# Attention numerators with tokens on partitions, quotients turned back by TensorE, and a planner with another product pace

## The chip, the cores and the metric

The kernel runs on one core of one Trainium2 chip. The metric is the device time of one execution in microseconds (us), lower is better; before the change the median of 3 runs is 940.74 us (940.22 to 941.93).

## The reference

```
def phi(x):                       # x: q or k, scaled by 64 ** -0.25
    proj = einsum('bhsd,md->bhsm', x, omega)
    h = proj - sum(x * x, -1) / 2
    return exp(h - max(h, -1)) / sqrt(m)
kv  = einsum('bhsm,bhsd->bhmd', k_p, v);  z = sum(k_p, axis=2)
num = einsum('bhsm,bhmd->bhsd', q_p, kv)
den = einsum('bhsm,bhm->bhs', q_p, z)[..., None] + 1e-06
x = (num / den) as 2304 tokens x 512
x = (silu(x @ w_gate) * (x @ w_val)) @ w_out        # 512 -> 1536 -> 512
x = g(x @ w_in) @ w_out2                            # 512 -> 2048 -> 512, g piecewise quadratic
```

Batch is 4, heads 8, sequence 576, head size 64, features m = 128. Everything is float32.

## The kernel before, in words

The 2304 tokens are cut into nine blocks of 256 (`TB`), numbered k; the eight heads into two halves of four heads, numbered d. So there are 18 pieces (k, d) of attention output.

**Attention.** `front` (L616 to L670) makes exp(features) of keys or queries with tokens on partitions: TensorE projects (L639), VectorE takes the negated maximum (L648), ScalarE the exponential (L661, or L665 on VectorE and L669). `k_group` multiplies these with the values, 65 columns a head: 64 values and a column of ones whose sum becomes z (L708). `kv_evac` copies the finished sums of a batch into `kvr`, once the 64 columns of kv, once z repeated over 64 columns. `q_group` turns the queries' features so that features lie on partitions (L779, TensorE transposes against the identity `ids`, copied to `q_t`).

**The piece that changes.** `num` makes the output of one piece with the kv sums as the stationary operand: for each of two head pairs it sends the 256 turned queries through `kvr`'s kv half and through its z half (L833, eight products of 256 columns; 16 shorter ones where a block crosses from one batch into the next, at k = 2, 4 and 6). So the numerator stands in one PSUM bank with head dimensions on partitions, and the denominator, repeated over 64 partitions, in another. `norm` inverts the denominator on VectorE: transpose in 32 x 32 blocks (L796), a strided sum that adds 1e-6 (L798), a reciprocal of 16 columns (L800), a transpose back (L801), and the product with the numerator (L805). The result `os` is split into a high and a low part (`x1s`, through `parts`) and stored to `x1d`.

**The two dense layers.** Each product is made of three matmuls (L403 to L405, high x high, high x low, low x high), 256 columns each. The first two sixths of layer one run as soon as a block is ready (`moe1`), between the pieces of attention. The rest runs in passes (`late_up`, `late_down`): `set_up` makes seven products a set in Strassen's manner on sums of input quarters, with partial sums copied from PSUM into the tile `eb` (`keep_bank`, the copy is L384 on ScalarE or L386 on VectorE) and added there (L1235); the products after them in the same bank wait for that copy. Weights come as raw 64-bit numbers: a transfer into `ws`, then L420 on ScalarE and L421 to L427 on VectorE make float32 of them (`to_f32`), a store to `w32` for later.

**What sets the order.** A planner (`Planner`) runs the whole program once while it is recorded: every step of every process gets a cost (`c_pe`, `c_act`, `c_dve`, fixed numbers) and a priority (the `PR_` numbers), and the time at which the planner's clock dispatches it fixes its place in its engine's queue. Engines take their queues strictly in that order, whatever the chip's real pace. `SLACK_D` is the time that `late_down` lets pass after an output row is ready before it plans the products on that row. All transfers are issued by SyncE (SP), also in planned order.

Of the kernel before, what the change touches and what calls it, by code (L numbers as in the profile page):

```python
# [19 lines left out]
F32 = mybir.dt.float32  # L20
F32R = mybir.dt.float32r
U32 = mybir.dt.uint32
AF = mybir.ActivationFunctionType
ALU = mybir.AluOpType
AX = mybir.AxisListType
# [3 lines left out]
P = 128  # L29
TB = 256  # L30
# [9 lines left out]
LEAN_A, LEAN_B, POOL_B = 0.97, -0.09, 5.00  # L40
ALT = 1.63

SLACK_D, SLACK_U = 3.0, 0.8

O_OFF, P_OFF, H_OFF = 32, 48, 48

NWL, NB1 = 7, 8
KINS, VINS, QINS, EBK, EBQ, N_QT = 3, 5, 2, 3, 2, 3
N_KL, N_QL, N_EL = 2, 1, 1

GROUPS = ((0,), (1, 2), (3, 4), (5, 6), (7, 8))

# [6 lines left out]
N_WT, N_XU = 3, 2  # L59
N_EB, N_GB, N_HL, N_HB, N_XI = 4, 2, 2, 1, 4  # L60

PR_K, PR_Q0, PR_Q = (0.32, 0.77, 0.91, 1.17), 0.17, 0.68
PR_C0, PR_C, PR_CS = 0.66, 1.02, 1.13
PR_W = 1.06
PR_BANK = 0.3
PR_FRONT = 0.35
PR_ST, PR_X, PR_E = 1.50, 0.74, 1.45
T_V, T_Q0, T_C0 = 3.0, 3.5, 7.0
N_GATE, N_CS = 1, 6
N_WS = 2  # L70

ORDER = (0, 1, 2, 3, 4)
# [61 lines left out]
class Planner:  # L134
# [24 lines left out]
    def set(self, ev):  # L159
        ev.done = True  # L160
        ev.src = self.src()
        for p in ev.waiters:
            self.after(p, ev.src)
            self.push(self.now, self.step, p, None)
        ev.waiters = []
# [93 lines left out]
def c_act(n, bias=False):  # L259
    return (115 + n) / 1200.0 + (0.05 if bias else 0.0)  # L260


def c_dve(n, psum=False, fast=False):
    return (66 + (n / 2 if fast else n)) / 960.0


def c_pool(n):
    return 0.11 + 0.00218 * n


def c_pe(n):
    return max(0.109, 0.0045 + n * 0.000442)


@with_exitstack
def performer_moe_kernel(ctx: ExitStack, tc: tile.TileContext, qX, kX, vX, om, ident,
                         w1, wo1, w2, wo2, out):
    nc = tc.nc
    pl = Planner()
# [4 lines left out]
    def bufs(pool, name, n, shape, dt=F32):  # L284
        return [pool.tile(shape, dt, tag=f"{name}{i}", name=f"{name}{i}") for i in range(n)]

    def ring(*a):
        return Ring(bufs(*a))
# [6 lines left out]
    bank = ring(psum, "bank", 8, [P, 512])  # L295
# [32 lines left out]
    osb = ring(keep, "os", 3, [P, 512])  # L328
# [5 lines left out]
    att_cm = tc.tile_pool(name="att", bufs=1, side="right", reuse_waits="tile")  # L334
    att = att_cm.__enter__()
    stat = ring(att, "st", 10, [P, 8, 4])
    rec = ring(att, "rec", 2, [P, 512])
    rect = ring(att, "rect", 1, [P, 16, 33])
    vin = ring(att, "vi", VINS, [P, 390])
    qts = ring(att, "qt", N_QT, [P, 2, 2, TB])  # L340
    ids = att.tile([P, P], F32, name="ids")
# [3 lines left out]
    ebufs = {False: ring(att, "ebk", EBK, [P, 2, 512]), True: ring(att, "ebq", EBQ, [P, 2, 512])}  # L345
    kin = ring(att, "ki", KINS, [P, 2, 512])
    qin = ring(att, "qi", QINS, [P, 2, 512])
    kvr = {(b, d): att.tile([P, 2, 2, P], F32, name=f"kvr{b}_{d}") for b in range(4) for d in range(2)}
    lent_cm = tc.tile_pool(name="lent", bufs=1, side="left", reuse_waits="tile")
    lent = lent_cm.__enter__()  # L350
    lent_ids = set()
# [1 line left out]
    def lend(rng, *a):  # L353
        for t in bufs(lent, *a):
            rng.free.append((t, None))
            lent_ids.add(id(t))
            lent_keep.append(t)
# [12 lines left out]
    lend(kin, "kl", N_KL, [P, 2, 512])  # L370
    lend(qin, "ql", N_QL, [P, 2, 512])
    lend(ebufs[False], "el", N_EL, [P, 2, 512])
    nc.gpsimd.memset(rect.free[0][0][:, :, 32:33], 1e-6)


    def dma(dst, src, nbytes):
        yield Op("SP", 0.06, lambda: nc.sync.dma_start(dst, src))
        yield Op("HW", 0.05, None)
        yield Op("DMA", nbytes / 330e3, None)

    def copy(dst, src, n, sbuf=True, scale=None):
        e = pl.pick(ACT=c_act(n), DVE=c_dve(n, fast=sbuf))
        if e == "ACT":
            yield Op("ACT", c_act(n), lambda: nc.scalar.activation(dst, src, AF.Copy, scale=1.0 if scale is None else scale))  # L384
        elif scale is None:
            yield Op("DVE", c_dve(n, fast=sbuf), lambda: nc.vector.tensor_copy(dst, src), sbuf)  # L386
        else:
            yield Op("DVE", c_dve(n, fast=sbuf), lambda: nc.vector.tensor_scalar(
                out=dst, in0=src, scalar1=scale, scalar2=None, op0=ALU.mult))
# [190 lines left out]
    halves = slice(0, 64), slice(64, P)  # L580

    def bank_pair():

        tok = yield Get(two_banks)
        b0 = yield Get(bank)
        b1 = yield Get(bank)
        pl.put(two_banks, tok)
        return b0, b1
# [30 lines left out]
    def front(xb, n, loads, is_q, rng):  # L619
# [13 lines left out]
        rank = pl.cur.rank  # L633
        pl.cur.rank = min(pl.cur.prio, PR_FRONT)

# [47 lines left out]
    def k_group(b, gs, kb, prev):  # L683
# [28 lines left out]
        for u in range(2 * n):  # L712
            i = 2 * gs[0] + u
            if i % 9 == 8:
                pl.spawn(kv_evac(b, i // 9), pl.cur.prio - 0.1)
# [22 lines left out]
    def kv_evac(b, d):  # L738
        kb = kv_bank.pop((b, d))
        kp = kb.rearrange("p (u c) -> p u c", c=P)  # L740
        kz = kvr[b, d].rearrange("p r a c -> p (r a) c")
        yield from copy(kz[:, :, 0:64], kp[:, :, 0:64], 256, False, 1.0 / P)
        yield from copy(kz[:, :, 64:P], kp[:, :, 64:65].to_broadcast([P, 4, 64]), 256, False, 1.0 / P)
        pl.put(bank, kb)
        pl.set(kv_ready[b, d])

# [41 lines left out]
            yield ev  # L788
        pl.spawn(num(k, d, q_t), pl.cur.prio - 0.05)

    def norm(pn, pd, rc, x):

        tt = yield Get(rect)
        st = yield Get(stat)
        s = st.rearrange("p a b -> p (a b)")
        yield Op("DVE", c_dve(512), lambda: nc.vector.transpose(out=tt[:, :, 0:32], in_=pd.rearrange("p (n c) -> p n c", c=32)))  # L796
        pl.put(bank, pd)
        yield Op("DVE", 0.105, lambda: nc.vector.tensor_reduce(out=s[:, 0:16], in_=tt[:, :, 0:33:32], axis=AX.X, op=ALU.add))  # L798
        pl.put(rect, tt)
        yield Op("DVE", 0.14, lambda: nc.vector.reciprocal(out=s[:, 16:32], in_=s[:, 0:16]))  # L800
        yield Op("DVE", c_dve(512), lambda: nc.vector.transpose(  # L801
            out=rc.rearrange("p (n c) -> p n c", c=32), in_=s[:, 16:32].unsqueeze(2).to_broadcast([P, 16, 32])))
        pl.put(stat, st)
        if pl.pick(DVE=c_dve(512), POOL=c_pool(512) + c_act(512) + ALT) == "DVE":
            yield Op("DVE", c_dve(512), lambda: nc.vector.tensor_tensor(out=x, in0=pn, in1=rc, op=ALU.mult))  # L805
            pl.put(bank, pn)
        else:
            yield Op("ACT", c_act(512), lambda: nc.scalar.activation(x, pn, AF.Copy))
            pl.put(bank, pn)
            yield Op("POOL", c_pool(512), lambda: nc.gpsimd.tensor_tensor(out=x, in0=x, in1=rc, op=ALU.mult))  # L810

    def num(k, d, q_t):
        yield x1_have[k]
        cuts = []
        t0 = k * TB
        while t0 < (k + 1) * TB:
            b = t0 // 576
            t1 = min((b + 1) * 576, (k + 1) * TB)
            cuts.append((b, t0 - k * TB, t1 - k * TB))
            t0 = t1  # L820
        for b, _, _ in cuts:
            yield kv_ready[b, d]
        x = yield Get(osb)
        rc = yield Get(rec)
        banks = yield from bank_pair()
        pl.cur.rank = min(pl.cur.prio, PR_FRONT)

        def mm():
            for r in range(2):
                for what in range(2):  # L830
                    for b, c0, c1 in cuts:
                        for a, h in enumerate(halves):
                            nc.tensor.matmul(banks[what][h, r * TB + c0:r * TB + c1], kvr[b, d][:, r, a, halves[what]],  # L833
                                             q_t[:, r, a, c0:c1], start=True, stop=True, skip_group_check=True)
        yield Op("PE", 1.88 if len(cuts) == 1 else 1.94, mm)
        pl.put(qts, q_t)
        yield from norm(*banks, rc, x)
        pl.put(rec, rc)
        pl.cur.rank = PR_Q
        yield from x1_split(k, d, x)  # L840
        yield from dma(half_block(x1d, k, d), x.rearrange("p (n t) -> p n t", n=2), P * 512 * 4)
        pl.put(osb, x)

    def half_block(t, k, d):

        return t[k // 2][:, 2 * d:2 * d + 2, (k % 2) * TB:(k % 2 + 1) * TB]

    def x1_split(k, d, x):
        xs = x1_tile[k]
        hi, lo = (xs[:, l, 2 * d:2 * d + 2].rearrange("p k t -> p (k t)") for l in range(2))  # L850
        yield from parts(hi, lo, x, 512)
        x1_cnt[k] = x1_cnt.get(k, 0) + 1
        if x1_cnt[k] == 2:
            pl.set(x1_ready[k])
# [808 lines left out]
```

## Time and profile before

| | |
|---|---|
| median of 3 runs | 940.74 us |
| the profiled execution | 939.58 us, its span 937.8 us |
| PE (TensorE matmuls) | 927.0 us busy, 99% |
| DVE (VectorE) | 787.0 us, 84% |
| ACT (ScalarE) | 509.2 us, 54% |
| POOL (GpSimd) | 65.1 us, 7% |
| PE's granted clock | 0.999 of full speed (2.4 GHz) |
| DMA | 147.68 MB, mean 157 GB/s |

The span is what the profiler covers of the profiled execution; 1.8 us of that execution lie outside it. The attention pieces lie in its first 232 us, mixed with products of the first layer from 47 us on; the rest is dense layers. A busy TensorE is counted from the start of a matmul to its modelled end, and these overlap, so a busy share of 100% hides short waits: the number of matmuls that start in a stretch tells more.

### The profile page before, as it was taken

What the parts mean: (1) busy time and instruction counts of PE and PEld (TensorE: products, weight loads), DVE (VectorE), ACT (ScalarE), POOL (GpSimd) and SP (SyncE); (2) the same over time, 40 slices, a digit from 0 to 9 for tenths busy, and PEclk for the clock granted to TensorE, in tenths of its full rate; (3) what the DMA queues carried; (4) which work ended last, traced back from release to release, by engine and by line L of the source; (5) the groups of instructions that cost most, each with busy time, mean ns of one, the idle gap of its engine ahead of it and who ended that gap; (6) DMA issues with size and microseconds to landing.
All of it is one profiled execution on the core that took longest, in us unless ns stands there. A gap on an engine that the chain in (4) does not pass through costs nothing.

```text
span 937.8 us, 22182 instructions
## 1 busy us (share of the span) xinstructions
PE 927.0 (99%) x8980; PEld 902.7 (96%) x8980; DVE 787.0 (84%) x1483; ACT 509.2 (54%) x1126; POOL 65.1 (7%) x57
## 2 busy tenths in 40 slices
PE   8999999999999999999999999999999999999998
PEld 7889899999999999999999999999999999999998
DVE  6899988778889999999989999997697678866553
ACT  7889975543446545564445465554455445544331
POOL 0332226222100000000000000000000000000000
PEclk9999999999999999999999999999999999999999
DMA  7667566555576366756745745442323031303022
GB/s 244 202 201 233 183 223 198 186 180 184 199 239 211 129 208 215 249 179 194 231 149 192 251 142 172 145 157 76 118 68 114 33 114 46 135 13 102 1 91 91
DMA packets 88663, 147.68 MB, mean 157 GB/s; under 512 B 8304, under 2 KB 43888, under 8 KB 88560
## 3 DMA queue, kind: packets, MB, share of 16 engines
q1 hardware_dynamic: 88560, 146.26, 47.8%
q8 instruction: 70, 1.15, 0.5%
q14 instruction: 33, 0.27, 0.1%
HBM read 103.24 MB, written 42.99 MB: 156 GB/s over the span
## 4 chain that ended last, share of the span: by engine, by line
PE 76%; DVE 15%; DMA 4%; issue 2%; ACT 2%; SPq 1%; DVEq 0%; ACTq 0%
PE bank L403 23%; PE bank L404 22%; PE bank L405 22%; PE bank L639 3%; PE bank L833 3%; PE bank L779 1%; PE bank L708 1%; DMA xq<-x2d 1%; DMA ws<-in_w_dram 1%; DVE st L648 1%; DVE x1s L396 1%; DVE wt L427 1%; DVE wt L425 1%; DMA ws<-in_wo_dram 1%; DVE xq L396 1%
## 5 line engine op out<-in xcount | busy, mean ns | idle before, releaser
L403 PE MATMUL bank<-x1s,w 128*128 128x256 f32 x492 | 137.4, 279 | 0.4 <-DVE eb L1235 0.4
L405 PE MATMUL bank<-x1s,w 128*128 128x256 f32 x492 | 136.1, 277 | 0.0
L404 PE MATMUL bank<-x1s,w 128*128 128x256 f32 x492 | 136.0, 276 | 0.0
L403 PEld LDWEIGHTS bank<-x1s,w 128*128 128x128 f32 x492 | 92.4, 188 | 1.6 <-DVE eb L1235 0.6
L405 PEld LDWEIGHTS bank<-x1s,w 128*128 128x128 f32 x492 | 92.5, 188 | 0.0
L404 PEld LDWEIGHTS bank<-x1s,w 128*128 128x128 f32 x492 | 92.4, 188 | 0.0
L403 PE MATMUL bank<-x1s,wb 128*128 128x256 f32 x286 | 79.2, 277 | 1.7 <-ACT eb L384 1.0
L384 ACT ACTIVATE x1s<-xq 128x512 fp32r<-128x512 f32 x80 | 50.2, 629 | 54.1 <-PE bank L405 23.2
L405 PE MATMUL bank<-x1s,wb 128*128 128x256 f32 x286 | 79.0, 276 | 0.0
L404 PE MATMUL bank<-x1s,wb 128*128 128x256 f32 x286 | 79.0, 276 | 0.0
L403 PE MATMUL bank<-x1s,wx 128*128 128x256 f32 x278 | 77.2, 278 | 1.0 <-ACT eb L384 1.0
L404 PE MATMUL bank<-x1s,wx 128*128 128x256 f32 x278 | 76.8, 276 | 0.0
L405 PE MATMUL bank<-x1s,wx 128*128 128x256 f32 x278 | 76.8, 276 | 0.0
L396 DVE TENSOR_TENSOR x1s<-xq,x1s 128x512 fp32r<-128x512 f32 x90 | 61.9, 687 | 9.0 <-ACT x1s L384 8.5
L384 ACT ACTIVATE eb<-bank 128x512 f32<-128x512 f32 x94 | 55.6, 591 | 23.6 <-PE bank L405 23.2
L420 ACT ACTIVATE wt<-ws 128x512 f32<-128x512 f32 x68 | 46.3, 686 | 35.4 <-DMA ws<-in_w_dram 18.3
L648 DVE TENSOR_REDUCE st<-bank 128x4 f32<-128x512 f32 (+1 forms) x76 | 47.9, 655 | 11.2 <-PE bank L639 11.2
L403 PEld LDWEIGHTS bank<-x1s,wb 128*128 128x128 f32 x286 | 53.7, 188 | 2.1 <-ACT eb L384 1.2
L384 ACT ACTIVATE hlr<-hb 128x512 fp32r<-128x512 f32 x53 | 33.4, 632 | 41.0 <-PE bank L404 26.2
L404 PEld LDWEIGHTS bank<-x1s,wb 128*128 128x128 f32 x286 | 53.7, 188 | 0.0
L405 PEld LDWEIGHTS bank<-x1s,wb 128*128 128x128 f32 x286 | 53.7, 188 | 0.0
L403 PEld LDWEIGHTS bank<-x1s,wx 128*128 128x128 f32 x278 | 52.2, 188 | 1.4 <-ACT eb L384 1.2
(256 smaller groups left out, 3341.6 us busy)
## 6 DMA issues: line engine op xcount, KB each, us to landing
ws<-in_w_dram SPq DMA_DIRECT2D x40, 512.0 KB, 4.7
ws<-in_wo_dram SPq DMA_DIRECT2D x28, 512.0 KB, 4.3
xq<-x1d SPq DMA_DIRECT2D x36, 256.0 KB, 4.2
xq<-x2d SPq DMA_DIRECT2D x36, 256.0 KB, 4.1
qi<-in_qX_dram SPq DMA_DIRECT2D x28, 256.0 KB, 3.8
ki<-in_kX_dram SPq DMA_DIRECT2D x22, 256.0 KB, 3.9
x1d<-os SPq DMA_DIRECT2D x18, 256.0 KB, 3.8
op<-os SPq DMA_DIRECT2D x18, 256.0 KB, 2.0
```

The lines of the kernel that those rows point to most:

```text
L384: yield Op("ACT", c_act(n), lambda: nc.scalar.activation(dst, src, AF.Copy, scale=1.0 if scale is None else scale))
L396: yield Op("DVE", c_dve(n), lambda: nc.vector.tensor_tensor(out=dst, in0=a, in1=b, op=op), True)
L403: nc.tensor.matmul(ps, l_hi, r_hi, start=first, stop=False, skip_group_check=shared)
L404: nc.tensor.matmul(ps, l_hi, r_lo, start=False, stop=False, skip_group_check=shared)
L405: nc.tensor.matmul(ps, l_lo, r_hi, start=False, stop=last, skip_group_check=shared)
L420: yield Op("ACT", 0.575, lambda: nc.scalar.activation(t, hw.bitcast(F32), AF.Abs))
L425: yield Op("DVE", c_dve(512), lambda: nc.vector.scalar_tensor_tensor(out=ti, in0=lw, scalar=29, in1=ti, op0=ALU.logical_shift_right, op1=A ...
L427: yield Op("DVE", c_dve(512), lambda: nc.vector.scalar_tensor_tensor(out=ti, in0=hw, scalar=0xC0000000, in1=ti, op0=ALU.bitwise_and, op1=A ...
L639: nc.tensor.matmul(banks[a][:, u * P:(u + 1) * P], xb[h, l, u * P:(u + 1) * P], r[h], start=first and (last or u == 0), stop=last, skip_gr ...
L648: yield Op("DVE", c_dve(256 * n), lambda: nc.vector.tensor_reduce(out=sv[:, a, units, 3 if by_pe else 0], in_=pv[a], axis=AX.X, op=ALU.max ...
L708: nc.tensor.matmul(kp[h, 2 * pr + a, 0:65], es[:, a, u * P + 64 * m:u * P + 64 * m + 64], v[:, 65 * a:65 * a + 65], start=(li == 0 and a = ...
L833: nc.tensor.matmul(banks[what][h, r * TB + c0:r * TB + c1], kvr[b, d][:, r, a, halves[what]], q_t[:, r, a, c0:c1], start=True, stop=True, ...
```

## The change

The numerators are computed with the operands exchanged. The turned queries become the stationary operand (64 tokens of one head at a time), and `kvr`, now 65 columns a head (kv and z side by side, one copy instead of two), is sent through them: 16 matmuls of 65 columns a piece, whatever batch border it crosses. So numerator and denominator stand with tokens on partitions: for each of the two banks (128 tokens each) VectorE adds 1e-6 to four columns, one reciprocal serves 8 columns, and one product a bank writes the quotients to `rec`. Four TensorE transposes turn them back, and a copy (16 of 18 on ScalarE) brings them to `os`. The tile `rect` and GpSimd's part in the quotient go.

The planner's price of a product changes (0.1177 to 0.1134 us for 256 columns), `SLACK_D` from 3.0 to 2.0, some priorities and start times, and three lent buffers become five (`N_KL`, `N_EL`).

```diff
-SLACK_D, SLACK_U = 3.0, 0.8
+SLACK_D, SLACK_U = 2.0, 0.8
-N_KL, N_QL, N_EL = 2, 1, 1
+N_KL, N_QL, N_EL = 3, 1, 2
-PR_K, PR_Q0, PR_Q = (0.32, 0.77, 0.91, 1.17), 0.17, 0.68
+PR_K, PR_Q0, PR_Q = (0.32, 0.9, 0.96, 1.0), 0.17, 1.01
-T_V, T_Q0, T_C0 = 3.0, 3.5, 7.0
-N_GATE, N_CS = 1, 6
+T_V, T_Q0, T_C0 = 3.84, 2.87, 5.5
+N_GATE, N_CS = 1, 3
...
 def c_pe(n):
-    return max(0.109, 0.0045 + n * 0.000442)
+    return max(0.109, n * 0.1134 / 256)
...
     def kv_evac(b, d):
-        kz = kvr[b, d].rearrange("p r a c -> p (r a) c")
-        yield from copy(kz[:, :, 0:64], kp[:, :, 0:64], 256, False, 1.0 / P)
-        yield from copy(kz[:, :, 64:P], kp[:, :, 64:65].to_broadcast([P, 4, 64]), 256, False, 1.0 / P)
+        yield from copy(kvr[b, d], kp[:, :, 0:65], 260, False, 1.0 / P)
...
-    def norm(pn, pd, rc, x):
+    def norm(pn, xt):
...
+        pv = [ps[:, 0:260].rearrange("p (h c) -> p h c", c=65) for ps in pn]
+        for t in range(2):
+            yield Op("DVE", 0.12, lambda: nc.vector.tensor_scalar(
+                out=s[:, 4 * t:4 * t + 4], in0=pv[t][:, :, 64], scalar1=1e-6, scalar2=None, op0=ALU.add))
+        yield Op("DVE", 0.12, lambda: nc.vector.reciprocal(out=s[:, 8:16], in_=s[:, 0:8]))
+        for t in range(2):
+            yield Op("DVE", c_dve(TB), lambda: nc.vector.tensor_tensor(
+                out=xt[:, t].rearrange("p (h c) -> p h c", c=64), in0=pv[t][:, :, 0:64],
+                in1=s[:, 8 + 4 * t:12 + 4 * t].unsqueeze(2).to_broadcast([P, 4, 64]), op=ALU.mult))
+            pl.put(bank, pn[t])
...
         def mm():
+            for t in range(2):
+                for h in range(4):
+                    for m, rows in enumerate(halves):
+                        nc.tensor.matmul(banks[t][rows, 65 * h:65 * h + 65], q_t[:, h // 2, h % 2, t * P + 64 * m:t * P + 64 * m + 64],
+                                         kvr[tiles[t][m], d][:, h], start=True, stop=True, skip_group_check=True)
+        yield Op("PE", 1.02, mm)
+        pl.put(qts, q_t)
+        yield from norm(banks, xt)
+        tp = yield Get(bank)
+
+        def trans():
             for r in range(2):
-                for what in range(2):
-                    for b, c0, c1 in cuts:
-                        for a, h in enumerate(halves):
-                            nc.tensor.matmul(banks[what][h, r * TB + c0:r * TB + c1], kvr[b, d][:, r, a, halves[what]],
-                                             q_t[:, r, a, c0:c1], start=True, stop=True, skip_group_check=True)
-        yield Op("PE", 1.88 if len(cuts) == 1 else 1.94, mm)
...
+                for t in range(2):
+                    nc.tensor.transpose(tp[:, r * TB + t * P:r * TB + (t + 1) * P], xt[:, t, r * P:(r + 1) * P], ids)
+        yield Op("PE", 0.55, trans)
+        pl.put(rec, xt)
+        x = yield Get(osb)
+        yield from copy(x, tp, 512, False)
```

How the queues change is read from the built programs. On PE, at the two pieces of the last token block (`bank<-qt,kvr` are the numerators and denominators, `hl,w` the dense layers' products), before:

```order
L405 MATMUL bank_64<-hl,w_114 128x256
L833 MATMUL bank_65<-qt_140,kvr_0_163 64x256 x2
L833 MATMUL bank_68<-qt_140,kvr_0_163 64x256 x2
L833 MATMUL bank_65<-qt_140,kvr_0_163 64x256 x2
L833 MATMUL bank_68<-qt_140,kvr_0_163 64x256 x2
L833 MATMUL bank_69<-qt_142,kvr_1_164 64x256 x2
```

and at the same place in the changed program (with `ids,rec`, the transposes, further down):

```order
L403 MATMUL bank_66<-hl,w_114 128x256
L819 MATMUL bank_70<-kvr_0_162,qt_140 64x65 x8
L819 MATMUL bank_64<-kvr_0_162,qt_140 64x65 x8
L819 MATMUL bank_68<-kvr_1_163,qt_141 64x65 x8
L819 MATMUL bank_67<-kvr_1_163,qt_141 64x65 x8
L401 MATMUL bank_66<-hl,w_115 128x256
...
L829 MATMUL bank_69<-ids,rec_132 128x128 x4
L401 MATMUL bank_65<-x1s_73,w_110 128x256
```

The transposes stand 21 and 33 dense matmuls behind the numerators, each group of four alone among them.

On DVE, the quotients of those two pieces, before:

```order
L796 STREAM_TRANSPOSE rect_134<-bank_68 128x16x32
L798 TENSOR_REDUCE st_126<-rect_134 128x16
L800 RECIPROCAL st_126<-st_126 128x16
L801 STREAM_TRANSPOSE rec_132<-st_126 128x512
L796 STREAM_TRANSPOSE rect_134<-bank_63 128x16x32
L805 TENSOR_TENSOR os_103<-bank_65,rec_132 128x512
L798 TENSOR_REDUCE st_131<-rect_134 128x16
```

and now:

```order
L793 TENSOR_SCALAR st_122<-bank_70 128x4
L793 TENSOR_SCALAR st_122<-bank_64 128x4
L795 RECIPROCAL st_122<-st_122 128x8
L793 TENSOR_SCALAR st_130<-bank_68 128x4
L797 TENSOR_TENSOR rec_132<-bank_70,st_122 128x256
L793 TENSOR_SCALAR st_130<-bank_67 128x4
L425 SCALAR_TENSOR_TENSOR wt_79<-ws_77,wt_79 128x512
L797 TENSOR_TENSOR rec_132<-bank_64,st_122 128x256
```

Both transposes and the 16-column sum are gone, and the product over 512 columns became two over 256.

Near the program's start SP's queue has the first queries ahead of the values of the first batch; before, they stood behind them:

```order
L377 DMA vi_138<-in_vX_dram 128x260
L377 DMA vi_139<-in_vX_dram 128x260
L377 DMA qi_155<-in_qX_dram 128x512
L377 DMA qi_156<-in_qX_dram 128x512
L377 DMA ws_76<-in_w_dram 128x1024
```

and now:

```order
L375 DMA ids<-in_ident_dram 128x128
L375 DMA qi_154<-in_qX_dram 128x512
L375 DMA qi_155<-in_qX_dram 128x512
L375 DMA vi_134<-in_vX_dram 128x260
L375 DMA vi_135<-in_vX_dram 128x260
```

Two query transfers moved ahead of the five value transfers.

## Rows read from the trace of the kernel before

**Rows 1.** The page's first part: engine, busy us, share of the span, instructions.

```profile
PE 927.0 (99%) x8980; PEld 902.7 (96%) x8980; DVE 787.0 (84%) x1483; ACT 509.2 (54%) x1126; POOL 65.1 (7%) x57
```

**Rows 2.** Windows (start:end length, busy of PE, PEld, DVE, ACT, POOL, PEclk, DMA share, GB/s).

```profile
75.00:100.00 25.00, 25.00 (x343) 22.43 (x344) 24.08 (x54) 23.45 (x100) 6.36 (x5) 1.00 0.67 220
250.00:600.00 350.00, 346.40 (x3035) 344.98 (x3035) 332.33 (x633) 183.09 (x343) 0.00 (x0) 1.00 0.58 190
600.00:900.00 300.00, 300.00 (x2649) 300.00 (x2649) 229.31 (x403) 145.36 (x260) 0.00 (x0) 1.00 0.27 89
```

**Rows 3.** Timeline of ACT and PE at 341 us (start, length, instruction, idle before).

```profile
341.00 0.67 ACT L420 ACTIVATE wt<-ws 128x512 f32<-128x512 f32 x1 [3.71 <-DMA ws<-in_wo_dram]
...
346.53 0.60 ACT L384 ACTIVATE eb<-bank 128x512 f32<-128x512 f32 x1
...
347.18 0.39 PE L403 MATMUL bank<-x1s,wx 128*128 128x256 f32 x1 [1.05 <-ACT eb L384]
```

**Rows 4.** Line L420: what ended ScalarE's idle time before it (us, times).

```profile
  DMA ws<-in_w_dram: 18.3, 14
  DMA ws<-in_wo_dram: 9.6, 5
```

**Rows 5.** Waits of PE in the whole span (us in total, times, longest).

```profile
PE bank L403 <- ACT eb L384: 2.4, 3, 1.0
PE bank L639 <- DMA qi<-in_qX_dram: 1.1, 1, 1.1
```

**Rows 6.** Timeline of PE at the last two pieces of attention.

```profile
227.88 0.28 PE L405 MATMUL bank<-hl,w 128*128 128x256 f32 x1
228.09 3.67 PE L833 MATMUL bank<-qt,kvr 128*64 128x256 f32 x32
231.69 0.39 PE L403 MATMUL bank<-hl,w 128*128 128x256 f32 x1
231.91 0.28 PE L404 MATMUL bank<-hl,w 128*128 128x256 f32 x1
```

**Rows 7.** Timeline of PE at 98 us, key features with values.

```profile
98.00 1.15 PE L708 MATMUL bank<-vi,ebk 128*64 128x65 f32 x32
99.08 0.39 PE L403 MATMUL bank<-x1s,w 128*128 128x256 f32 x1
```

**Rows 8.** Timeline of PE at 139 us and 183 us, transposes and a pair across batches.

```profile
138.87 1.97 PE L779 MATMUL bank<-ids,ebq 128*128 128x128 f32 x16
140.59 0.36 PE L403 MATMUL bank<-hl,wx 128*128 128x256 f32 x1
140.79 0.28 PE L404 MATMUL bank<-hl,wx 128*128 128x256 f32 x1
...
183.30 3.75 PE L833 MATMUL bank<-qt,kvr 128*64 128x192 f32 x64
186.98 1.97 PE L779 MATMUL bank<-ids,ebq 128*128 128x128 f32 x16
```

**Rows 9.** Lines by form, DVE, 0 to 236 us (busy us, mean ns, idle before).

```profile
L801 DVE STREAM_TRANSPOSE rec<-st 128x512 f32<-128x512 f32 x18 | 12.6, 702 | 0.3
L796 DVE STREAM_TRANSPOSE rect<-bank 128x512 f32<-128x512 f32 x18 | 12.5, 696 | 4.3 <-PE bank L833 4.2
L805 DVE TENSOR_TENSOR os<-bank,rec 128x512 f32<-128x512 f32 x17 | 11.5, 677 | 0.5
L653 DVE TENSOR_REDUCE st<-st 128x8 f32<-128x16 f32 x36 | 5.7, 163 | 0.3
L800 DVE RECIPROCAL st<-st 128x16 f32<-128x16 f32 x18 | 4.5, 248 | 0.2
L798 DVE TENSOR_REDUCE st<-rect 128x16 f32<-128x32 f32 x18 | 3.2, 177 | 0.2
L665 DVE TENSOR_TENSOR ebk<-bank,st 128x256 f32<-128x256 f32 x2 | 0.8, 412 | 0.0
```

**Rows 10.** Lines by form, ACT, 0 to 236 us.

```profile
L384 ACT ACTIVATE kvr<-bank 128x256 f32<-128x256 f32 x14 | 5.1, 376 | 0.0
L384 ACT ACTIVATE xi<-bank 128x512 f32<-128x512 f32 x5 | 3.0, 591 | 0.7 <-PE bank L405 0.7
```

More of the change, by code (lines that the diff above doesn't have):

```diff
@@ L60 @@
 N_EB, N_GB, N_HL, N_HB, N_XI = 4, 2, 2, 1, 4
-PR_K, PR_Q0, PR_Q = (0.32, 0.77, 0.91, 1.17), 0.17, 0.68
-PR_C0, PR_C, PR_CS = 0.66, 1.02, 1.13
+PR_K, PR_Q0, PR_Q = (0.32, 0.9, 0.96, 1.0), 0.17, 1.01
+PR_C0, PR_C, PR_CS = 0.66, 1.08, 0.7
 PR_W = 1.06
 PR_BANK = 0.3
-PR_FRONT = 0.35
+PR_FRONT = 0.2
 PR_ST, PR_X, PR_E = 1.50, 0.74, 1.45
-T_V, T_Q0, T_C0 = 3.0, 3.5, 7.0
-N_GATE, N_CS = 1, 6
+T_V, T_Q0, T_C0 = 3.84, 2.87, 5.5
+N_GATE, N_CS = 1, 3
 N_WS = 2
@@ L336, in performer_moe_kernel @@
     stat = ring(att, "st", 10, [P, 8, 4])
-    rec = ring(att, "rec", 2, [P, 512])
-    rect = ring(att, "rect", 1, [P, 16, 33])
+    rec = ring(att, "rec", 2, [P, 2, TB])
     vin = ring(att, "vi", VINS, [P, 390])
@@ L347, in performer_moe_kernel @@
     qin = ring(att, "qi", QINS, [P, 2, 512])
-    kvr = {(b, d): att.tile([P, 2, 2, P], F32, name=f"kvr{b}_{d}") for b in range(4) for d in range(2)}
+    kvr = {(b, d): att.tile([P, 4, 65], F32, name=f"kvr{b}_{d}") for b in range(4) for d in range(2)}
     lent_cm = tc.tile_pool(name="lent", bufs=1, side="left", reuse_waits="tile")
@@ L372, in performer_moe_kernel @@
     lend(ebufs[False], "el", N_EL, [P, 2, 512])
-    nc.gpsimd.memset(rect.free[0][0][:, :, 32:33], 1e-6)
     def dma(dst, src, nbytes):
@@ L789, in q_group @@
         pl.spawn(num(k, d, q_t), pl.cur.prio - 0.05)
-    def norm(pn, pd, rc, x):
-        tt = yield Get(rect)
+    def norm(pn, xt):
         st = yield Get(stat)
         s = st.rearrange("p a b -> p (a b)")
[L796 to L802, printed above, removed]
-        pl.put(stat, st)
[L804 to L810, printed above, removed]
@@ L812, in num @@
+        pl.put(stat, st)
     def num(k, d, q_t):
         yield x1_have[k]
[L814 to L821, printed above, removed]
+        tiles = []
+        for t in range(2):
+            i = 2 * k + t
+            tiles.append([(i * P + 64 * m) // 576 for m in range(2)])
+        for b in sorted(set(tiles[0] + tiles[1])):
@@ L822, in num @@
             yield kv_ready[b, d]
-        x = yield Get(osb)
-        rc = yield Get(rec)
+        xt = yield Get(rec)
         banks = yield from bank_pair()
@@ L828, in mm @@
         def mm():
-            for r in range(2):
-                for what in range(2):
-                    for b, c0, c1 in cuts:
-                        for a, h in enumerate(halves):
-                            nc.tensor.matmul(banks[what][h, r * TB + c0:r * TB + c1], kvr[b, d][:, r, a, halves[what]],
-                                             q_t[:, r, a, c0:c1], start=True, stop=True, skip_group_check=True)
-        yield Op("PE", 1.88 if len(cuts) == 1 else 1.94, mm)
-        pl.put(qts, q_t)
-        yield from norm(*banks, rc, x)
-        pl.put(rec, rc)
+            for t in range(2):
[8 more added lines that the diff above has]
+        def trans():
+            for r in range(2):
+                for t in range(2):
+                    nc.tensor.transpose(tp[:, r * TB + t * P:r * TB + (t + 1) * P], xt[:, t, r * P:(r + 1) * P], ids)
[3 more added lines that the diff above has]
+        yield from copy(x, tp, 512, False)
+        pl.put(bank, tp)
         pl.cur.rank = PR_Q
```

## Prediction

> **What bounds the kernel now.** I read the page's busy shares first, then windows, then PE's waits and its timeline around the pieces that change. TensorE is busy for 99% of the span and no other engine above 84% [rows 1]. The reader should see there only that TensorE is the candidate; since its busy time hides short waits, the windows decide. In the last 300 us of dense layers 2649 matmuls start, 8.83 a us, 0.1132 us each, with the clock at 1.00 (2.4 GHz) [rows 2]. At that pace 250 to 600 us would hold 3090; it holds 3035, so 55 x 0.1132 = **6.3 us** are lost there to waits. DVE is 95% busy there, 332.33 of 350, but the one stall of 1.05 us that the timeline shows in full has another cause: ScalarE stood 3.71 us in its queue for a raw weight that had not landed, the copy of a PSUM bank to `eb` behind it came late, and the product that needs the bank waited [rows 3]. ScalarE waits so 19 times, 27.9 us in all [rows 4]; PE shows 2.4 us of waiting on that copy [rows 5], the rest of the 6.3 being short. In the attention stage PE starts work without visible gaps from 75 to 100 us, with DVE and ACT both above 90% [rows 2]. So what shortens the program is (a) work taken off TensorE, anywhere, and (b) waits of TensorE in the middle of the dense layers. VectorE time alone is worth little: it is hidden under TensorE.
>
> **(a) TensorE's work.** Removed: two pieces take 231.69 - 228.09 = 3.60 us, 1.80 each [rows 6]; 18 x 1.80 = 32.4 us (pairs across a batch border take 3.68, from 183.30 to 186.98 [rows 8]; I keep 1.80). Added, numerators: 16 matmuls of 65 columns with a 128 x 64 stationary operand are, form for form, the key product of 32 records that takes 99.08 - 98.00 = 1.08 us [rows 7]; 18 x 1.08 = 19.4. Added, transposes: 16 take 140.59 - 138.87 = 1.72, 0.107 each [rows 8]; 72 x 0.107 = 7.7.
>
> Going from one kind of matmul to another costs something: 0.21 us from the last product to the first numerator and 0.22 for the first product after them, where 0.113 is the rule [rows 6], so 0.10 each; and 0.20 for the first product after transposes [rows 8], 0.09. Counted in both built orders, changes of the operand's shape (64 columns, 64 rows, full) go from 97 to 90, -0.7 us; returns from transposes straight to products from 4 to 16, 12 x 0.09 = +1.1. Sum: -32.4 + 19.4 + 7.7 + 0.4 = **-4.9 us**. The far bound: each group of four transposes costs 18 x (4 x 0.107 + 0.10 + 0.09) = 11.1 instead of 7.7 + 0.4; then the sum is -1.9. I take -4.9, since most groups stand next to the queries' transposes and pay no change of their own.
>
> A short moving operand shows its weight load where that is not hidden. Pairs across a border load twice as many operands (64 records against 32) for the same columns, and take 3.68 instead of 3.60 [rows 6, 8]: 0.0025 us a load, so loads are hidden. The Trainium skill ("TensorE: Matmul & The Clock Gate", section LDWEIGHTS) speaks against the change: a load takes its columns over 1.2 GHz, 53 ns for 64. If that paced the 32 records, a piece would take an estimated 1.71 us instead of 1.08 and this sum would be +6.4 instead of -4.9. The trace does not agree: 1.08 over 32 is 34 ns a record.
>
> **VectorE and ScalarE.** A piece loses 0.696 + 0.177 + 0.248 + 0.702 + 0.677 = 2.50 us on DVE and gains two products of 256 columns (0.412 each), two four-column sums and a reciprocal of 8 columns, which I bound between 0.163 and 0.248 each [rows 9]: 1.3 to 1.6. That is about 18 x 1.0 = 18 us less. ScalarE gains 16 copies of 0.591 and loses nine of the 14 halves of `kvr` at 0.376 [rows 10]: +9.5 - 3.4 = +6 us; the new order has 20 accumulating squares fewer there, which I leave out. All this is under TensorE's work: worth 0 directly. The cover is gone if TensorE waits for a quotient; the transposes stand 21 and 33 matmuls (2.4 and 3.7 us) behind the numerators, and the chain before them is 1.5 us of work, so it should hold.
>
> **(b) Waits.** The planner priced a product at 0.1177 us; the chip does 0.1132. So before, each plan was 4% slower than the chip's TensorE, and the 27.9 us of ScalarE's waits sit in such a plan; with 0.1134 copies and weight conversions stand nearer to where TensorE needs them. But the transfers are late for another reason, their own landing, and `SLACK_D` takes a microsecond of margin from every row. Bounds: all 6.3 us recovered, or as much again lost. I take **-2.0**, a third of the recovery, since only the copies' places and not the transfers get better. At the start, TensorE's 1.1 us wait for the first queries [rows 5] should go as their transfers move ahead of the values; but the values then come later to the first key product, which has been moved behind 72 projections; bounds -1.1 and +1.1, I take **-0.5**. SP issues as many transfers as before, in another order; GpSimd loses one product and a fill, hidden. Three more lent buffers only let key transfers start sooner.
>
> **Sum.** -4.9 - 2.0 - 0.5 = -7.4 us on the profiled execution's 939.58, which is 1.16 below the median of 940.74; from the median: **933.3 us**. About 0.2% (1.9 us) is what a measurement here tells from no change.
>
> **Rivals.**
> - *All stalls go.* -4.9 - 6.3 - 1.1 = -12.3: 928.4 us. For it: one price, wrong by 4%, stood behind every place in the queues. Against: the stall in rows 3 came from a transfer. Chance 0.10.
> - *Only the work counts, at its far bound.* Transposes in groups of four pay both changes and the plan is no better: -1.9 to -4.9 with stalls as before, centre -3: 937.7. For it: 16 returns to products instead of 4. Chance 0.15.
> - *Slower: ScalarE's queue blocks.* The place is the weight conversion in ScalarE's queue, between 250 and 600 us [rows 3, 4]: with tighter plans each of the 19 late transfers holds an `eb` copy and PE about 1 us. 19 instead of 6.3 lost is +12.7; with -5.4, the sum is +7.3: 948.0. It decides from 12 such stalls on (6.3 + 5.4 = 11.7 us lost). Against it: ScalarE is idle for nearly half of that stretch. Chance 0.09.
> - *Slower: loads are not hidden.* If the two 64-column halves of the array did not overlap, a record would cost twice 34 ns: 18 x 1.08 = 19.4 more, -7.4 + 19.4 = +12: 952.7. Against it stands the same form in rows 7. The 53 ns of the Trainium skill's "TensorE: Matmul & The Clock Gate" (section LDWEIGHTS) would give an estimated 944.6. Chance 0.03.
> - *It does nothing measurable:* gains of (a) given back in waits at the start, where the first dense product comes later; 940.7. Chance 0.03.
>
> **How the numbers follow.** The forecast has 0.60, its own range 930 to 937. Faster by over 0.2% is below 938.9: the forecast, the first rival and some 0.08 of the second, 0.78. Within 0.2%: 0.07 of the second and 0.03, 0.10. Slower: 0.12. The range leaves out both slower rivals (0.12), some of the first rival below 928 (0.04) and of the last (0.03): 928.0 to 939.8.
>
> **What would show it.** Right: numerators at 1.08 us a piece and transposes at about 0.43 in the timeline; the last transposes end about 3 us before 231.7; DVE's busy sum falls by about 18 us; 250 to 600 us holds more than 3035 matmuls, near 3050; the idle time of the first query projection is gone. Wrong: records of the numerators above 40 ns; PE waits on the transposes for `rec`; fewer than 3000 matmuls in 250 to 600 us, with ScalarE's waits on `ws` before the `eb` copies.

## Result and the profile after

The changed kernel takes 932.43 us (median of 6 runs, 930.35 to 934.02) against 940.8 of the kernel before in the same comparison: ratio 0.9912, 95% interval 0.9899 to 0.9925. That is 8.4 us faster; forecast were 7.4 us and 933.3. The profiled execution took 930.35 us, its span is 928.6, 9.2 us shorter than the span before.

The windows of the changed kernel (columns as in [rows 2]):

```profile
75.00:100.00 25.00, 25.00 (x429) 23.27 (x429) 23.84 (x58) 21.19 (x78) 3.98 (x3) 1.00 0.68 216
250.00:600.00 350.00, 347.89 (x3056) 347.05 (x3055) 329.08 (x625) 188.46 (x352) 0.00 (x0) 1.00 0.57 187
600.00:900.00 300.00, 300.00 (x2649) 300.00 (x2648) 228.26 (x406) 140.15 (x251) 0.00 (x0) 1.00 0.28 91
```

From 250 to 600 us 3056 matmuls start where 3035 did [rows 2]: 21 x 0.1132 = 2.4 us fewer lost. From 600 us on nothing changed, 2649 in both.

TensorE's timeline at the last two pieces of attention, which answers to [rows 6]:

```profile
221.88 2.09 PE L819 MATMUL bank<-kvr,qt 128*64 128x65 f32 x64
223.90 0.38 PE L401 MATMUL bank<-hl,w 128*128 128x256 f32 x1
...
226.41 0.60 PE L829 MATMUL bank<-ids,rec 128*128 128x128 f32 x4
226.76 0.36 PE L401 MATMUL bank<-x1s,w 128*128 128x256 f32 x1
226.96 0.28 PE L402 MATMUL bank<-x1s,w 128*128 128x256 f32 x1
...
228.62 0.37 PE L401 MATMUL bank<-x1s,w 128*128 128x256 f32 x1
```

Two pieces of numerators take 223.90 - 221.88 = 2.02 us, 1.01 each, where they took 1.80. Four transposes alone among products take 0.35 and cost 0.09 on the way back (0.20 instead of 0.113 from L401 to L402). So at this place a piece costs 1.01 + 0.44 = 1.45, 0.35 less than before; if all 18 did so it would be 6.3 us. Not all do: twelve pieces run in pairs like these, six alone at 0.98 to 1.09, and most groups of transposes stand next to other attention work, where they take 0.41 to 0.59. Summed over the whole timeline, each run from its start to the next one's, the old numerators take 32.8 us, the new ones 18.4 and the transposes 8.1; with 7 x 0.09 = 0.6 for returns to products that is 5.7 us less.

The whole account fits. Attention's last matmul is followed by a product at 228.62 us, where it was 231.69 [rows 6]; by the built orders 852 matmuls of the dense layers stand ahead of that point now, 819 did. So the stage up to there gained 3.07 + 33 x 0.1132 = 6.8 us, and with the 2.4 of the dense layers that is the 9.2 of the spans. Of the 6.8, 5.7 are TensorE's work as summed above; the rest is waits, the start and order, and isn't divided further here.

The same count can be made for every kernel below. Take the start of the first product behind attention's last matmul and subtract 0.1132 us for each dense matmul that started ahead of it: what remains is the attention stage's own time, 139.0 us before (231.69 - 819 x 0.1132) and 132.2 now.

The lines of VectorE in the first 236 us, which answer to [rows 9], and the copy on ScalarE:

```profile
L797 DVE TENSOR_TENSOR rec<-bank,st 128x256 f32<-128x256 f32 x36 | 14.4, 415 | 0.2
L793 DVE TENSOR_SCALAR st<-bank 128x4 f32<-128x4 f32 x36 | 4.9, 151 | 1.3 <-PE bank L819 1.2
L795 DVE RECIPROCAL st<-st 128x8 f32<-128x8 f32 x18 | 3.4, 194 | 0.2
...
L382 ACT ACTIVATE os<-bank 128x512 f32<-128x512 f32 x16 | 9.6, 603 | 6.6 <-PE bank L829 5.9 <-issue 0.4
```

A piece's quotients cost 2 x 0.415 + 2 x 0.151 + 0.194 = 1.33 us on VectorE instead of 2.50.

What still holds TensorE: its waits in the whole span, and the largest stall of the changed kernel's dense layers, ScalarE and PE at 382 us:

```profile
PE bank L401 <- ACT eb L382: 2.1, 2, 1.3
PE bank L1566 <- DVE hb L1564: 1.5, 1, 1.5
PE bank L829 <- DVE rec L797: 0.7, 1, 0.7
PE bank L829 <- DVE os L384: 0.7, 1, 0.7
PE bank L637 <- DVE ebk L663: 0.6, 1, 0.6
```

```profile
381.81 0.66 ACT L418 ACTIVATE wt<-ws 128x512 f32<-128x512 f32 x1 [1.96 <-DMA ws<-in_w_dram]
382.38 0.58 ACT L382 ACTIVATE eb<-bank 128x512 f32<-128x512 f32 x1
...
383.01 0.38 PE L401 MATMUL bank<-x1s,w 128*128 128x256 f32 x1 [1.33 <-ACT eb L382]
```

The stall at 382 us is that of [rows 3] in another place: a raw weight lands late, the bank's copy stands behind it in ScalarE's queue, TensorE waits.

### The profile page after: what moved, and what is told of

Same layout as the page of the kernel before. It is cut to its first block, busy times and chain, and to the rows that moved or that the text cites. A ratio compares the mean times of both kernels' runs of the same rounds, so it can differ in the third digit from the quotient of the medians.

```text
span 928.6 us, 22636 instructions
## 1 busy us (share of the span) xinstructions
PE 919.4 (99%) x9244; PEld 904.7 (97%) x9244; DVE 773.9 (83%) x1499; ACT 508.9 (55%) x1085; POOL 63.0 (7%) x54
## 4 chain that ended last, share of the span: by engine, by line
PE 92%; DVE 5%; DMA 1%; ACT 1%; issue 1%; SPq 0%; DVEq 0%; ACTq 0%
PE bank L401 27%; PE bank L402 26%; PE bank L403 26%; PE bank L637 5%; PE bank L706 2%; PE bank L819 2%; PE bank L775 2%; PE bank L829 1%; DMA ws<-in_w_dram 1%; DVE st L646 1%; DMA xq<-x2d 0%; PE bank L1566 0%; DMA xp<-x2q 0%; DVE w L394 0%; DVE xq L394 0%
## 5 line engine op out<-in xcount | busy, mean ns | idle before, releaser
L401 PE MATMUL bank<-x1s,w 128*128 128x256 f32 x492 | 137.6, 280 | 1.3 <-ACT eb L382 1.3
L402 PE MATMUL bank<-x1s,w 128*128 128x256 f32 x492 | 136.0, 277 | 0.0
L401 PEld LDWEIGHTS bank<-x1s,w 128*128 128x128 f32 x492 | 92.5, 188 | 2.2 <-ACT eb L382 1.5
L402 PEld LDWEIGHTS bank<-x1s,w 128*128 128x128 f32 x492 | 92.4, 188 | 0.0
L382 ACT ACTIVATE x1s<-xq 128x512 fp32r<-128x512 f32 x86 | 53.9, 628 | 51.0 <-PE bank L403 33.2
L401 PE MATMUL bank<-x1s,wb 128*128 128x256 f32 x286 | 79.0, 276 | 0.0
L402 PE MATMUL bank<-x1s,wb 128*128 128x256 f32 x286 | 79.0, 276 | 0.0
L401 PE MATMUL bank<-x1s,wx 128*128 128x256 f32 x278 | 77.2, 278 | 0.8 <-ACT eb L382 0.7
L402 PE MATMUL bank<-x1s,wx 128*128 128x256 f32 x278 | 76.8, 276 | 0.0
L418 ACT ACTIVATE wt<-ws 128x512 f32<-128x512 f32 x68 | 46.1, 680 | 24.8 <-DMA ws<-in_w_dram 15.3
L1231 DVE TENSOR_TENSOR gb<-bank,eb 128x512 f32<-128x512 f32 x64 | 43.8, 685 | 13.0 <-PE bank L403 12.8
L401 PEld LDWEIGHTS bank<-x1s,wb 128*128 128x128 f32 x286 | 53.7, 188 | 0.0
L402 PEld LDWEIGHTS bank<-x1s,wb 128*128 128x128 f32 x286 | 53.7, 188 | 0.0
L401 PEld LDWEIGHTS bank<-x1s,wx 128*128 128x128 f32 x278 | 52.2, 188 | 1.3 <-ACT eb L382 1.2
```

The source lines that it names most:

```text
L401: nc.tensor.matmul(ps, l_hi, r_hi, start=first, stop=False, skip_group_check=shared)
L402: nc.tensor.matmul(ps, l_hi, r_lo, start=False, stop=False, skip_group_check=shared)
L418: yield Op("ACT", 0.575, lambda: nc.scalar.activation(t, hw.bitcast(F32), AF.Abs))
```

## Experiments

Twelve kernels were run, each against the kernel before on the same chip (its medians 941.1 to 941.3 there). "Stage" is the attention stage's own time, counted as above; "lost" is (3090 - matmuls that start from 250 to 600 us) x 0.1132 us (55 x 0.1132 = 6.2 before, where the prediction has 6.3). Both come from one profiled execution of each kernel, and executions of one kernel differ by 0.5 to 7.2 us; differences in microseconds are between medians unless the text says otherwise. In every kernel the profiled span is stage plus lost plus 792.5 to 793.6 us, so the two columns hold nearly all that differs.

| kernel | median us | ratio, 95% interval | stage us | lost, 250 to 600 us |
|---|---|---|---|---|
| before | 941.1 | | 139.0 | 6.2 |
| the change | 932.43 | 0.9912 (0.9899 to 0.9925) | 132.2 | 3.9 |
| new price alone | 938.05 | 0.9971 (0.9958 to 0.9984) | 137.9 | 3.6 |
| new numerators alone | 939.31 | 0.9987 (0.9971 to 1.0002) | 136.6 | 6.8 |
| numerators + price | 934.21 | 0.9928 (0.9914 to 0.9942) | 135.6 | 4.6 |
| all numbers, old numerators | 936.88 | 0.9961 (0.9949 to 0.9973) | 138.6 | 5.4 |
| the change, old price | 940.41 | 0.9995 (0.9981 to 1.0010) | 134.5 | 12.2 |
| the change, slack 3.0 | 932.68 | 0.9908 (0.9895 to 0.9921) | 132.7 | 5.2 |
| the change, price 0.1091 | 931.33 | 0.9889 (0.9866 to 0.9913) | 132.4 | 2.9 |
| numerators twice | 947.46 | 1.0065 (1.0050 to 1.0080) | 150.5 | 2.7 |
| transposes back twice | 941.82 | 1.0006 (0.9992 to 1.0019) | 140.6 | 8.4 |
| VectorE's transposes back | 934.76 | 0.9931 (0.9917 to 0.9946) | 134.2 | 6.2 |
| all transfers dearer | 951.25 | 1.0098 (1.0078 to 1.0117) | 132.2 | 24.2 |
| conversions planned 1.5 us later | 928.19 | 0.9861 (0.9842 to 0.9881) | 131.1 | 2.5 |

**The parts of the change.** Four kernels. The first is the kernel before with one line:

```diff
-    return max(0.109, 0.0045 + n * 0.000442)
+    return max(0.109, n * 0.1134 / 256)
```

> The kernel before with the planner's price of a product alone set to that of the change (0.1134 us instead of 0.1177 for 256 columns). My theory: the price is what recovers the waits between 250 and 600 us, some 2 to 2.4 us of 940.8: 938.6, with about 3056 matmuls in that stretch instead of 3035. Rival (the transfers of raw weights land late whatever the plan): 940.8 within 1, about 3035 matmuls.

The second is the changed kernel with every number of the kernel before; the third the kernel before with every number of the change:

```diff
-SLACK_D, SLACK_U = 2.0, 0.8
-N_KL, N_QL, N_EL = 3, 1, 2
...
-T_V, T_Q0, T_C0 = 3.84, 2.87, 5.5
...
-    return max(0.109, n * 0.1134 / 256)
+SLACK_D, SLACK_U = 3.0, 0.8
+N_KL, N_QL, N_EL = 2, 1, 1
...
+T_V, T_Q0, T_C0 = 3.0, 3.5, 7.0
...
+    return max(0.109, 0.0045 + n * 0.000442)
```

> The new numerators, with every planner number of the kernel before (price, slack, priorities, start times, lent buffers). My theory: TensorE's work counts in full, -4.9 us, and the waits stay: 935.9 (934 to 938). Rival A (the gain is the new plan's, the numerators save little once their transposes stand alone): 939 or more. Rival B (VectorE's 18 us of relief is what counts, so nearly all of the 8.4 us comes with the numerators): 932.5 to 933.5.

> The old numerators with every planner number of the change. My theory: the waits' share alone, -2 to -3.5 us: 937.3 to 938.8. Rival A: most of the 8.4 us, 934 or less. Rival B: 940.8 or more, since the numbers were fitted to the other work.

The fourth is the change with the old line of `c_pe`.

> The change with only the planner's price of a product put back to 0.1177. My theory: the 2 to 2.4 us of waits come back: 934.6 (934 to 936), about 3035 matmuls between 250 and 600 us. Rival (the place of the stalls is chance, set by the transfers): 932.4 within 1.

Measured: the price alone gives 3.0 us (ratio 0.9971), as expected, with 3058 matmuls from 250 to 600 us. The numerators alone give 1.8 us where my theory said 4.9, and a ratio of 1 lies within their interval. All numbers without the numerators give 4.2 us, a little more than my range. And the change without the price gives nothing that shows: 940.41, 8 us above the change, where my theory had 934.6 and the rival 932.4. So the parts don't add up: what the numerators are worth depends on the price. The trace of the numerators alone shows where theirs went: of the 6.8 us that the change takes off the attention stage they take off 2.4 (136.6 against 139.0), and from 50 to 150 us TensorE waits 2.4 us for ScalarE, where the kernel before shows a single wait of 0.3; the other 2 us aren't in the list of waits.

Waits of PE from 50 to 150 us, numerators alone:

```profile
PE bank L401 <- ACT ebk L659: 1.3, 1, 1.3
PE bank L401 <- ACT qt L382: 0.8, 1, 0.8
PE bank L401 <- ACT ebq L659: 0.3, 1, 0.3
```

The change with the old price loses most in the dense layers. Its windows, and ScalarE and PE at 371 us:

```profile
250.00:600.00 350.00, 342.39 (x2982) 340.35 (x2982) 332.37 (x636) 177.75 (x331) 0.00 (x0) 1.00 0.57 192
```

```profile
371.11 0.66 ACT L418 ACTIVATE wt<-ws 128x512 f32<-128x512 f32 x1 [3.32 <-DMA ws<-in_w_dram]
371.67 0.58 ACT L382 ACTIVATE eb<-bank 128x512 f32<-128x512 f32 x1
...
372.31 0.39 PE L401 MATMUL bank<-x1s,wx 128*128 128x256 f32 x1 [2.37 <-ACT eb L382]
```

2982 matmuls, 74 fewer than the change's 3056: that is 8.4 of the 10.8 us between the two profiled spans (939.4 and 928.6); the other 2.3 lie in the attention stage. The stall at 371 us is the slower rival's mechanism, a late weight in front of an `eb` copy. It costs more than its wait, since behind it the granted clock falls from 1.00 to 0.50:

```profile
374.00:376.00 2.00, 2.00 (x11) 2.00 (x11) 2.00 (x5) 1.34 (x3) 0.00 (x0) 0.50 0.00 0
```

```profile
374.53 0.41 PE L401 MATMUL bank<-xur,wx 128*128 128x256 f32 x1
374.75 0.41 PE L402 MATMUL bank<-xur,wx 128*128 128x256 f32 x1
```

From 373.68 to 377.09 us sixteen products start 0.213 us apart instead of 0.113, 1.6 us more. The total of 12.2 us lost is past the 11.7 where I had put the rival's point of decision, but that all of it has this cause is not shown: TensorE's waits in this stretch add up to 7.6 us, of which 3.5 (two waits) are on an `eb` copy by ScalarE. In the change the longest such stall is the 1.33 us at 382 us, and the clock stays at 1.00 there. But the price alone doesn't keep such stalls away: with all new numbers and the old numerators ScalarE waits 4.22 us for a weight before 357.94 us, TensorE 1.95 for the `eb` copy that stands four places behind it, and the clock falls as well:

```profile
360.48 0.39 PE L403 MATMUL bank<-xur,w 128*128 128x256 f32 x1 [1.95 <-ACT eb L384]
```

```profile
362.00:364.00 2.00, 2.00 (x11) 2.00 (x11) 1.80 (x4) 1.23 (x3) 0.00 (x0) 0.50 0.60 233
```

That profiled execution is one of the three longest of its ten (939.04 us, the median is 936.88).

**Numerators and price, and the slack.** The first is the changed kernel with the old numbers but for `c_pe`; the second the change with `SLACK_D` at 3.0.

> The new numerators and the new price of a product; slack, priorities, start times and lent buffers as in the kernel before. My theory now: the numerators take 4.9 us off TensorE but the old plan loses some 3.4 us of it in waits between 50 and 150 us; the price gives back the dense layers' 2.7 us. 941.1 - 4.9 + 3.4 - 2.7 = 936.9 (935.5 to 938.5), with about 8 us lost between 50 and 150 us. Rival (the price repairs the attention stage too, the other numbers do nothing): 933 or less.

> The change with SLACK_D alone put back to 3.0. My theory: at the right price the slack is worth little either way: 932.4 within 1.5. Rival (the shorter slack is what shortens the dense layers): 935 or more. Second rival (the shorter slack costs waits, as it did with the old price): 930.5 or less.

Numerators and price take 934.21: lower than my theory's range, near the rival that the price repairs the attention stage too. At the right price the numerators are worth 938.05 - 934.21 = 3.8 us, and 936.88 - 932.43 = 4.5 with all other numbers; at the old price 1.8 (941.1 to 939.31). The other numbers are worth 934.21 - 932.43 = 1.8 us between medians, which is not clear of noise, since the two intervals overlap; in the two traces the stage goes from 135.6 to 132.2. The slack is worth nothing that shows (932.68), as expected.

**Is TensorE's work paid in full?** The change with each piece's numerators made twice, then with its transposes back made twice:

```diff
-            for t in range(2):
+            for t in (0, 1, 0, 1):
...
-        yield Op("PE", 1.02, mm)
+        yield Op("PE", 2.04, mm)
```

> The change with every numerator product made twice (16 more matmuls of 65 columns a piece; the second run overwrites the first). My theory: TensorE bounds the stage, so all of it is paid: 18 x 1.05 to 1.08 = 18.9 to 19.4 us, 951.3 to 951.8 (within 1.5). Rival (waits of the attention stage hide part of it): 946 or less.

> The change with the four transposes that turn a piece's quotients back made twice (the second run overwrites the first). My theory: 72 more transposes at 0.107 us are 7.7 us of TensorE work, of which the numerators' doubling says some 85% shows: 938.5 to 940.5. Rival (they fill time in which TensorE waits for quotients): 935 or less.

TensorE's timeline of the doubled numerators:

```profile
120.05 3.95 PE L819 MATMUL bank<-kvr,qt 128*64 128x65 f32 x128
123.94 1.31 PE L775 MATMUL bank<-ids,ebq 128*128 128x128 f32 x10
```

A pair takes 3.89 us instead of 2.02, so nine pairs are 16.8 us more, less than the 19 I had put in; 15.0 show in the median, below my theory's band and above the rival's. In the traces the stage grows by 18.4 and the dense layers lose 1.1 less. Doubled transposes are 7.7 us and cost 9.4 in the median, above my range; the stage grows by 8.4, and in that profile the dense layers lose 8.4 instead of 3.9. So work on TensorE is paid at about its length, and each new order of the queues adds or takes an amount of 1 to 5 us in the dense layers.

**VectorE's relief.** The change with the two block transposes a piece put back on a tile that nothing reads; this adds work and leaves the result alone:

```diff
         yield from norm(banks, xt)
+        pl.spawn(again(), pl.cur.prio)
...
+    def again():
+        z = yield Get(dead)
+        for _ in range(2):
+            yield Op("DVE", c_dve(512), lambda: nc.vector.transpose(out=z[:, 1], in_=z[:, 0]))
+        pl.put(dead, z)
```

> The change with the two 32 x 32 block transposes a piece that VectorE no longer makes put back on a tile that nothing reads, planned at the piece's priority: 18 x 1.40 = 25 us more VectorE work before 236 us. My theory: VectorE's relief by itself is worth next to nothing: 932.4 to 934. Rival B (it is part of the gain): 936 or more, with PE's waits between 50 and 150 us up by 3 us or more.

25 us of VectorE work cost 2.3 us, a little over my theory's band and short of the rival's; the two ratios' intervals overlap. In the traces the stage takes 134.2 us instead of 132.2, and the dense layers, where none of the added work stands, lose 6.2 instead of 3.9. So the 21 us that the quotients no longer take on VectorE are worth a tenth of their length or so, and since a new order alone moves as much, it is not shown that they are worth anything.

**Is it the right price, or a low one?** The change with a price as far below the chip's pace as the old one was above it:

```diff
-    return max(0.109, n * 0.1134 / 256)
+    return max(0.109, n * 0.1091 / 256)
```

> The change with the planner's product priced as much below the chip's pace as the old price lay above it (0.1091 us against 0.1132 measured; old 0.1177, new 0.1134). My theory: what counts is that the price is the chip's pace; a plan that runs ahead of TensorE costs too, though less, because engines that are early do not hold TensorE: 933.5 to 936. Rival (a lower price only favours the engines that feed TensorE, the lower the better): 932 or less.

931.33: my theory of the right pace falls. The rival, 932 or less, holds. A price that is 4% too low costs nothing here; a price 4% too high costs 8 us in the same kernel. My reading, which no run tests by itself: a plan in which TensorE is too fast makes the other engines serve it early, and early copies hold nobody.

**Late weights.** First every transfer's price was raised:

```diff
-        yield Op("DMA", nbytes / 330e3, None)
+        yield Op("DMA", nbytes / 220e3, None)
```

> The change with the planner's price of a transfer raised by half (220 instead of 330 KB a us, so that a 512 KB weight is planned at 3.9 us instead of 3.1; the trace's median is 4.6). My theory: what is left of the waits between 250 and 600 us comes from weights that land after ScalarE's turn, so some 1 to 2 us go: 930.5 to 931.5, and ScalarE waits less for raw weights than its 21.6 us. Rival (the remaining waits are spread over many causes): 932.4 within 1.5, or slower.

951.25, 19 us slower than the change. TensorE's longest waits in the dense layers (250 to 600 us) of that kernel, and what ended ScalarE's idle time before L418 in its whole span:

```profile
PE bank L402 <- DVE x1s L394: 5.4, 4, 3.2
PE bank L401 <- ACT xur L382: 3.1, 2, 2.2
PE bank L402 <- DVE xur L394: 3.0, 3, 2.0
```

```profile
  DMA ws<-in_w_dram: 1.8, 1
```

ScalarE hardly waits for weights any more (1.8 us, where the change has 21.6), but TensorE now waits for its own input units `x1s` and `xur`. My reading, not tested by itself: in the plan the transfers of inputs became the limit, and everything that they feed was queued late. The edit changed the place of every transfer, so it doesn't answer the question, and the last kernel moves the weights' conversion alone:

```diff
     def to_f32(st, src, t):
         yield from dma(st, src, 524288)
+        yield 1.5
```

> The change with a raw weight's conversion planned 1.5 us later than the transfer's planned landing (3.1 us planned, 4.6 in the trace); no other transfer's price is touched. My theory: the stalls of TensorE on the eb copies stand behind ScalarE's waits for raw weights, so those waits (21.6 us in the change) fall below 8 us, the 2.7 us lost between 250 and 600 us fall to about 1, and the time to 930.5 to 931.5. Rival (the stalls come from the copies' own order against PE and move elsewhere): 932.4 within 1.5, with ScalarE's waits for weights down all the same.

928.19 us, 928.0 to 928.46 over four runs: 4.2 us below the change, and the intervals of the two ratios don't overlap; it is below my theory's 930.5 as well. Waits of ScalarE for raw weights from 250 to 600 us, of the change:

```profile
ACT wt L418 <- DMA ws<-in_w_dram: 12.0, 6, 5.1
ACT wt L418 <- DMA ws<-in_wo_dram: 5.4, 7, 2.3
```

and of this kernel, with PE's waits in its span:

```profile
ACT wt L419 <- DMA ws<-in_w_dram: 7.5, 6, 2.6
ACT wt L419 <- DMA ws<-in_wo_dram: 2.9, 4, 1.0
```

```profile
PE bank L1567 <- DVE hb L1565: 1.4, 1, 1.4
PE bank L401 <- ACT eb L382: 0.9, 2, 0.6
PE bank L638 <- ACT ebq L660: 0.3, 1, 0.3
PE bank L638 <- ACT ebk L660: 0.2, 1, 0.2
```

The longest waits are shorter (2.6 us instead of 5.1) and TensorE waits 0.9 us on `eb` instead of 2.1. Over the whole span ScalarE still waits 21.9 us for weights, 21.6 in the change, so that part of my expectation failed: what counts is how long one wait is and what stands behind it, not the sum. The gain is also larger than these waits; 1.4 us lie in 250 to 600 us (3068 matmuls against 3056; the 2.7 us lost that my expectation starts from is 3.9 by this count), the rest of the profiled difference of 2.4 in the attention stage (131.1 against 132.2), and the change's profiled execution took 930.35 us, below its median of 932.43. That the later conversion makes the kernel faster is shown; that it does so through these waits alone is not.

## Why the prediction was right, point by point

- **What bounds it.** TensorE, and its waits in the dense layers: held. Work added to TensorE was paid at about its length, work added to VectorE at a tenth or less.
- **(a), -4.9 us.** TensorE's own work fell by 5.7 us. The term of the numerators was too high: 1.08 is the price of a run of 32 records with both its ends, and the sum paid the ends once more as changes of shape; in pairs a piece takes 1.01, and all 18 take 18.4 us instead of 19.4. The transposes with their returns take 8.7, and the removed work was 32.8 instead of 32.4. The stage gained 6.8, start and waits included. But "anywhere" was too simple: between medians the term is 3.8 to 4.5 us at the new price and 1.8 at the old one. That the numerators need the new plan to be worth their length was in no step of mine.
- **The cover.** It held but for 0.7 us: one group of transposes waits for `rec`, which the prediction had named as a sign of being wrong, and another waits as long for `os`.
- **VectorE and ScalarE at 0.** Nearly: 25 us of VectorE work put back cost 2.3. VectorE's busy sum fell by 13.1 us (787.0 to 773.9), not 18: the quotients take 21.6 us less in the first 236 us (44.3 to 22.7), and other steps, spread over many lines, take 8.5 more. ScalarE's sum stayed (509.2 to 508.9) instead of rising by 6: its copies of `os` take 9.6 us, and the accumulating squares that I had left out are 20 fewer and take 9.4 less.
- **(b), -2.0 us.** 2.4 in the trace of the change; 3.0 for the price alone, whose trace shows 2.6 in the dense layers and 1.0 in the attention stage. The price alone moves only places in the queues, which agrees with the cause I gave, the copies' places, though late weights still cost the new numbers a long stall with the old numerators; what I said of `SLACK_D` did not hold: at the new price 2.0 and 3.0 are the same.
- **The start, -0.5 us.** TensorE's wait for the first queries [rows 5] is gone from its list. What that is worth by itself wasn't tried. The lent buffers are two more, not three.
- **The sum.** 7.4 us were forecast and 8.4 measured, and each term is near its size in the change. But the terms do not act apart as the sum has them: tried alone, price and numerators give 3.0 and 1.8 us. That they came out together at the forecast is partly luck, since the change happened to bring both.
- **Rivals.** The late weight before an `eb` copy exists and is dear; the changed kernel with the old price loses 12.2 us, part of it by this. My price for it was wrong: I counted 19 late transfers between 250 and 600 us, but only 11 of the 19 waits of [rows 4] lie there, and a long stall can cost the clock too. Loads that are not hidden: excluded, since a record takes 2.02 / 64 = 32 ns where that rival needed 68. The Trainium skill ("TensorE: Matmul & The Clock Gate", section LDWEIGHTS) gives an estimated 53 ns for a load of 64 columns; the trace does not agree that this paces the records.
- **Still open:** which of the remaining numbers carry the 1.8 us besides price and slack, if that difference is real; and why the last kernel gains more than the waits that it removes.

## What to carry to other kernels

When one engine bounds a program and the queues are laid out by a planner, try a price of that engine's steps at or just below the chip's pace: in this kernel 4% too high cost up to 8 us of 932, 4% too low nothing. Test a change of work and a change of plan each alone before you credit either, since here the work was worth 1.8 us in the old plan and about 4 in the new one. And look for what stands behind a late transfer in an in-order queue: planning each raw weight's conversion 1.5 us later was worth 4.2 us, while making all transfers dearer in the plan cost 19.

## What the runs showed of the hardware

- With a 128 x 64 stationary operand and 65 moving columns a run of 32 records takes 1.08 us [rows 7], of 64 records 2.02 and of 128 records 3.89. The differences, 0.94 for 32 and 1.87 for 64, are 29 ns a record each; so about 0.15 us of every run belongs to its two ends, and the 34 ns a record of the prediction had a share of that.
- The granted clock was 0.50 (1.2 GHz) from 374 to 376 us in the change with the old price, after TensorE had stood idle for 2.37 us and run again for 1.4; products then started 0.213 us apart instead of 0.113 until 377.09. With all transfers dearer, where TensorE had stood idle for 2.25 and 2.04 us with one product between, it was 0.93 on average over 50 us:

```profile
400.00:450.00 50.00, 44.33 (x357) 43.43 (x356) 46.44 (x91) 26.12 (x49) 0.00 (x0) 0.93 0.57 186
```

- How much one kernel's executions differ goes in part with that clock. Of ten with all numbers and the old numerators, the three of 939.0 us and more had a mean granted clock of 0.998, the seven of 937.3 and less 0.999 or 1.000. It doesn't go with the time lost: all transfers dearer lost the most and its six executions lie within 1.2 us.
